# Widening the narrow matmuls of a Fourier, gating and experts kernel to the whole TensorE array

## The chip, the cores and the metric

The kernel runs on one core of a Trainium2 chip. The metric is the device time of one execution in microseconds, from a median over several runs. Engines are named as the profile names them: PE is TensorE's matmul, PEld TensorE's weight load, DVE VectorE, ACT ScalarE, POOL GpSimd and SP SyncE, whose queue issues most of the DMAs.

## The reference, cut to what matters

```python
def reference(x, moe_w1, moe_w2, moe_w3, moe_w_out, moe2_expert_emb, moe2_tau, moe2_w1, moe2_w2):
    X = np.fft.fft(np.fft.fft(x, axis=1), axis=2).real      # x: 8 x 3072 x 256
    t = X.reshape(8 * 3072, 256)
    h = ((t @ moe_w1) * (t @ moe_w2)) @ moe_w3               # 256 -> 1024 -> 1024
    t = h @ moe_w_out                                        # 1024 -> 256
    tn, en = normalised(t), normalised(moe2_expert_emb)
    logits = tn @ en.T / moe2_tau                            # 8 experts
    e = argmax(logits); g = softmax(logits)[e]
    return g * (relu(t @ moe2_w1[e]) @ moe2_w2[e])           # one expert for each token
```

The real part of a 2D transform is symmetric, so half the rows are worked out and the other half follow from sums and differences of the same products.

## The kernel before, in words

Three stages follow one another. Products in float32 are made of three products of split operands: each operand is a high and a low part in the format `fp32r`, and the terms high by high, high by low and low by high are added in PSUM (`three`, `prod`, line 122).

**The transform** (`dft`). For each of 8 batches and 3 parts of the sequence (`KORD`), DVE and POOL fold the rows of `x` to sums and differences, ACT and DVE split them, and PE multiplies them with tables (`accumulate`, tile `acc`). One batch ends with one more term: 2 special rows (`spc`, 2 x 128) times a row of alternating signs (`pm`, 2 x 386). Feature 128, the middle of the spectrum, has no partner and goes the same way for all batches at once (`feature128`): its stationary tiles have 8 columns, one for each batch (`h8`, `l8`, and 2 rows by 8 columns in `x8`). Beside the transform a generator, `side`, prepares the weights; at its end `open_p1` loads the first data of the next stage.

**The middle** (`mid`). 24 chunks of 512 transform columns. A chunk has 8 steps, one for each 128 of the 1024 hidden features (`f`). A step is `stage_b` and `stage_c`. `stage_b` makes four PSUM tiles: `p0`, `q0`, `p1`, `q1`, each of three matmuls of 512 columns. `p1` has a fourth term, a rank-one correction for feature 128: the stationary operand is `wr`, 3 rows by 128 columns of the tile `wrx`, the moving one `ur`, 3 rows by 512 columns. DVE turns the tiles into `ps`, `a`, `b` and `g` (7 instructions a step; for `i` = 1 ACT copies `ps`). `just` splits one block of the chunk before into `jh` (ACT) and `jl` (POOL), and `stage_c` multiplies such a block with `wh` and `wl` (24 matmuls of 264 columns, tile `pc`, one PSUM buffer, which ACT copies to `xs`). Once a chunk, `choose` and `place` work out which expert each token goes to: a chain of some 30 small DVE instructions (`nrm`, `n8q`, `ohot`, `df`, up to `idx`), one ACT instruction (`ex`) and 9 small matmuls; then POOL sends 8 indirect DMAs (`scatter`, `dx`). In the first third, `presplit` also splits the experts' weights (`et`, `eh`, `el`). A small ninth job, `mini`, runs in chunk 0 with 8 matmuls of 3 rows and 8 columns (`umr`).

**The experts** (`experts`): tiles of 256 tokens, each with its expert's weights; nothing of the change lies there.

The order in which instructions stand on each engine is planned ahead of the run by the tile framework, from the order in the text, the tiles' dependences and its own idea of durations; only `experts` has its SyncE order written by hand. So on an engine, work of a later step can stand ahead of an earlier one. Each engine then runs its list in order.

Of the kernel before, what the change touches and what calls it, by code (L numbers as in the profile page):

```python
# [8 lines left out]
F32 = mybir.dt.float32  # L9
F32R = mybir.dt.float32r  # L10
# [8 lines left out]
NB, S, D, F, E = 8, 3072, 256, 1024, 8  # L19
N = NB * S  # L20
H = S // 2
CH = 512
# [37 lines left out]
def fourier_experts(  # L60
# [21 lines left out]
    nc = tc.nc  # L82
# [5 lines left out]
    dspx = tc.dram_tile([NB, 2, 130], F32, name="dspx")  # L88
    du128f = tc.dram_tile([NB, H + 2], F32, name="du128f")
    dwr = tc.dram_tile([3, F], F32, name="dwr")  # L90
# [64 lines left out]
    def load_uv(c, p, raw, pool):  # L155
        b, j = divmod(c, H // CH)
        sl = slice(j * CH, j * CH + CH)
        ru = raw.tile([128, CH], F32, tag="ru", name="ru")
        nc.sync.dma_start(out=ru, in_=du[b, :, sl])
        rv = raw.tile([128, CH], F32, tag="rv", name="rv")  # L160
        nc.sync.dma_start(out=rv, in_=dv[b, :, sl])
        ur = pool.tile([3, CH], F32R, tag=f"ur{p}", name="ur")
        ub = pool.tile([128, CH], F32, tag=f"ub{p}", name="ub")
        nc.sync.dma_start(out=ur[0:1, :].bitcast(F32), in_=du128[b, 0:1, sl])
        nc.sync.dma_start(out=ur[1:3, :].bitcast(F32), in_=du128[b, :, sl])
        nc.sync.dma_start(out=ub, in_=du128f[b:b + 1, sl].to_broadcast([128, CH]))
        return ru, rv, ur, ub
# [3 lines left out]
    def open_p1():  # L171
# [4 lines left out]
        p1["l"] = p1["w"][:, 4 * F:8 * F].rearrange("p (a f) -> p a f", f=F)  # L176
        p1["raw"], p1["uv"] = pool("uvr", left2), pool("uv0", left3)
        ld = load_uv(0, 0, p1["raw"], p1["uv"])
        for q in range(4):
            nc.sync.dma_start(out=p1["h"][:, q, :].bitcast(F32), in_=dwc[0, :, q, :])  # L180
            nc.sync.dma_start(out=p1["l"][:, q, :].bitcast(F32), in_=dwc[1, :, q, :])
        wrx = p1c.tile([128, 4 * XW], F32R, name="wrx")
        p1["wr"] = wrx[0:3, 0:F]
        p1["x"] = wrx.rearrange("p (a c) -> p a c", c=XW)
        nc.scalar.dma_start(out=p1["wr"].bitcast(F32), in_=dwr)
        p1["uh"] = p1c.tile([128, NB], F32R, name="umh")
# [253 lines left out]
def dft(nc, tc, ctx, pz, split, prod, three, x, x128, xsp, tables, p1, du, dv, du128, du128f, dsp, dspx, side):  # L440
# [13 lines left out]
    tl = tb.tile([128, 3, TW], F32R, name="tl")  # L454
    pm = tb.tile([2, 386], F32R, name="pm")

# [31 lines left out]
    load_table(KORD[1], 1)  # L488
    nc.gpsimd.dma_start(out=pm, in_=t_pm)
    ps_ = [wk.tile([128, 4, D + 1], F32, name=f"p{i}_") for i in range(2)]  # L490
# [86 lines left out]
    def fetch_sp(b):  # L577
        if b < NB:
            a = wk2.tile([1, 4, 128], F32, tag="spa", name="spa")
            nc.scalar.dma_start(out=a, in_=dsp[b:b + 1, :, 0:128])  # L580
            c = wk2.tile([2, 128], F32R, tag="spc", name="spc")
            nc.scalar.dma_start(out=c.bitcast(F32), in_=dspx[b, :, 0:128])
            spb[b] = (a, c)
# [7 lines left out]
    def tabs(v, slot, k):  # L591
# [8 lines left out]
        ]  # L600

    def accumulate(ps, rows, v, k, hi, lo, extra, slots=(0, 1, 2, 3)):
        for slot in slots:
            for g, th, tl, w in tabs(v, slot, k):
# [5 lines left out]
                o = ps[g][:rows, 0:w]  # L610
                prod(o, three(hi[:, slot, :], lo[:, slot, :], th, tl), begin, end and extra_ is None)
                if extra_ is not None:
# [11 lines left out]
    def feature128():  # L624
        xm = wk.tile([128, 3, 8, NB], F32, name="xm")
        nc.scalar.dma_start(out=xm, in_=x128)
        x8 = wk.tile([2, NB], F32R, name="x8")
        cm = wk.tile([128, 3, 4, NB], F32, name="cm8")
# [6 lines left out]
        gt(out=um_[:, :, 0, :], in0=dm[:, :, 0, :], in1=dm[:, :, 1, :], op=ALU.add)  # L635
        gt(out=um_[:, :, 1, :], in0=dm[:, :, 0, :], in1=dm[:, :, 1, :], op=ALU.subtract)
        with nc.allow_non_contiguous_dma(reason="a few numbers"):
            nc.sync.dma_start(out=x8.bitcast(F32), in_=dspx[:, :, 128].rearrange("b h -> h b"))
            nc.sync.dma_start(out=um_[0:1, 0, 3, :], in_=dsp[:, 1:2, 128].rearrange("b h -> h b"))
        h8 = wk.tile([128, 3, 4, NB], F32R, name="h8")  # L640
        l8 = wk.tile([128, 3, 4, NB], F32R, name="l8")
        yield
        split(h8, l8, um_, lo_eng=nc.gpsimd)
        yield
        for g, c, w in GROUPS:
            ps = {g: pz.tile([128, 512], F32, tag="z", name="p8")}
            for k in KORD:
                accumulate(ps, NB, 0, k, h8[:, k], l8[:, k], x8)
            n = w + 1 if g == 0 else w
# [21 lines left out]
    for i, (b, k) in enumerate(seq):  # L671
        if k == KORD[0]:
            fetch_sp(b + 1)
            pu = dict(enumerate(banks(4)))
        accumulate(pu, 128, 0, k, *ku.pop(i), spb[b][1])
        if k == KORD[-1]:
# [6 lines left out]
        if k == KORD[0]:  # L683
            pv = dict(enumerate(banks(2)))
        accumulate(pv, 128, 1, k, *kv[i], None, (0, 1))
        if k == KORD[-1]:
# [3 lines left out]
        if k == KORD[-1]:  # L690
            pw = dict(zip((2, 3), banks(2)))
            for q in range(3):
                accumulate(pw, 128, 1, KORD[q], *kv.pop(i - 2 + q), None, (2, 3))
            evacuate(pw, dv, b, GROUPS[2:4])
# [5 lines left out]
def mid(  # L700
# [14 lines left out]

    uvs = [p1["uv"], uv1]
    load_uv = lambda c: p1["load"](c, c % 2, p1["raw"], uvs[c % 2])
    split_uv = lambda c, ld: p1["split"](ld, c % 2, uvs[c % 2])
# [166 lines left out]
    def mini():  # L885
        umr = ro.tile([3, NB], F32R, tag="umr", name="umr")
        umb = ro.tile([128, NB], F32, tag="umb", name="umb")
# [500 lines left out]
```

## Time and profile before

| | |
|---|---|
| median of 3 runs | 2789.34 us (2785.59 to 2789.74) |
| profiled execution, span from first to last instruction | 2776.7 us |
| what lies around the span, median less span | 12.6 us |
| PE busy in the span | 2660.2 us |
| PEld busy in the span | 2411.1 us |
| DVE busy in the span | 1700.2 us |
| rank-one matmuls (3 rows) | 192 |
| special-row matmuls (2 rows) | 8, and 1 in feature 128 |
| matmuls with 8 stationary columns | 54 |

The profile page shows the span, not the whole time of that execution; the 12.6 us is worked out against the median. Busy times of PE are modelled, since matmuls overlap; the distance between the starts of two matmuls says more than their durations. An entry in square brackets in a timeline is the idle time of that engine before the instruction, and who ended it.

### The profile page before, as it was taken

The numbers are of one execution on the slowest core, as the hardware profiler recorded it, in microseconds if no ns is written. First come the engines' busy times: TensorE is split into PE (matmuls) and PEld (weight loads), VectorE is DVE, ScalarE is ACT, GpSimd is POOL, SyncE is SP. The second block draws the span as 40 slices with busy tenths as digits, with TensorE's granted clock in tenths as the row PEclk, the third lists the DMA queues.
The fourth block names the chain that finished last, engine by engine and source line by source line (L and its number), as shares of the span: only waits on it lengthen the run. The fifth ranks groups of instructions, "written<-read, shape, count | busy, mean of one in ns | idle before, by whom it ended". The sixth has DMA issues, their size and how long they took to land. (4 is left out here: it accounts for less than half of the span.)

```text
span 2776.7 us, 48845 instructions
## 1 busy us (share of the span) xinstructions
PE 2660.2 (96%) x18661; PEld 2411.1 (87%) x18661; DVE 1700.2 (61%) x3322; ACT 1054.6 (38%) x2069; POOL 1073.0 (39%) x741
## 2 busy tenths in 40 slices
PE   4998899999999999999999999999999999999998
PEld 3788677777788888878878899999999999999998
DVE  7999399999887887887887762232323222222222
ACT  3554244444434334334333433333333333333332
POOL 5455345565565565565555421111111111111111
PEclk7999799999999999999999999999999999999999
DMA  6766535455111011011010265111111422111110
GB/s 245 245 225 205 186 103 184 153 190 185 58 43 39 28 41 40 28 41 41 28 41 22 99 242 199 47 46 47 47 47 47 164 104 104 47 47 47 47 47 21
DMA packets 114249, 265.07 MB, mean 95 GB/s; under 512 B 16843, under 2 KB 55929, under 8 KB 109148
## 3 DMA queue, kind: packets, MB, share of 16 engines
q1 hardware_dynamic: 84670, 195.58, 21.5%
q0 software_dynamic: 19440, 51.35, 5.2%
q10 hardware_dynamic: 9902, 14.98, 1.5%
q8 instruction: 148, 2.42, 0.4%
q14 instruction: 89, 0.73, 0.1%
HBM read 521.17 MB, written 106.77 MB: 226 GB/s over the span
## 5 line engine op out<-in xcount | busy, mean ns | idle before, releaser
L1071 DVE SCALAR_TENSOR_TENSOR hl<-pd,hh 128x512 fp32r<-128x512 f32 x396 | 273.9, 692 | 779.4 <-ACT hh L1070 779.3
L115 POOL TENSOR_TENSOR jl<-g,jh 128x1024 fp32r<-128x1024 f32 x184 | 441.2, 2399 | 412.9 <-ACT jh L112 334.1
L1086 POOL DMA_INDIRECT out<-o,x x192 | 187.9, 978 | 913.0 <-ACT o L1085 894.4
L122 PE MATMUL pc<-wh,jh 128*128 128x264 f32 x1536 | 441.2, 287 | 15.9 <-ACT xs L799 14.0
L122 PE MATMUL pc<-wh,jl 128*128 128x264 f32 x1536 | 439.2, 286 | 7.4 <-POOL jl L115 7.4
L122 PE MATMUL pc<-wl,jh 128*128 128x264 f32 x1536 | 436.6, 284 | 0.0
L1067 PE MATMUL pd<-xh,wt 128*128 128x256 f32 x2400 | 428.9, 278 | 0.0
L1083 PE MATMUL po<-wt,hh 128*128 128x256 f32 x2400 | 424.1, 280 | 0.0
L112 ACT ACTIVATE jh<-g 128x1024 fp32r<-128x1024 f32 x192 | 203.4, 1059 | 469.9 <-PE pc L122 451.9
L1067 PEld LDWEIGHTS pd<-xh,wt 128*128 128x128 f32 x2400 | 369.2, 188 | 0.0
L1070 ACT ACTIVATE hh<-pd 128x512 fp32r<-128x512 f32 x396 | 237.0, 599 | 336.6 <-PE pd L1067 336.6
L1083 PEld LDWEIGHTS po<-wt,hh 128*128 128x128 f32 x2400 | 364.4, 188 | 0.0
L122 PE MATMUL q<-vh,wc 128*128 128x512 f32 x768 | 326.5, 427 | 13.9 <-ACT a L778 9.5
L1083 PE MATMUL po<-wt,hl 128*128 128x256 f32 x1200 | 334.1, 278 | 0.0
L1067 PE MATMUL pd<-xl,wt 128*128 128x256 f32 x1200 | 333.2, 278 | 0.0
L122 PEld LDWEIGHTS pc<-wh,jh 128*128 128x128 f32 x1536 | 290.4, 189 | 35.3 <-ACT xs L799 26.3
L122 PE MATMUL p<-uh,wc 128*128 128x512 f32 x768 | 307.4, 401 | 3.2 <-DVE ps L765 3.1
L122 PEld LDWEIGHTS pc<-wh,jl 128*128 128x128 f32 x1536 | 289.9, 189 | 12.2 <-POOL jl L115 12.0
L122 PEld LDWEIGHTS pc<-wl,jh 128*128 128x128 f32 x1536 | 290.6, 189 | 6.9
L780 DVE TENSOR_TENSOR b<-ps,q 128x512 f32<-128x512 f32 x384 | 249.0, 688 | 66.0 <-PE q L122 47.6
L783 DVE TENSOR_TENSOR g<-a,b 128x512 f32<-128x512 f32 x384 | 247.4, 679 | 6.3 <-POOL a L780 6.3
L1085 ACT ACTIVATE o<-po,x 128x256 f32<-128x256 f32 x192 | 91.3, 475 | 415.1 <-PE po L1083 415.0
(327 smaller groups left out, 5199.5 us busy)
## 6 DMA issues: line engine op xcount, KB each, us to landing
wt<-dex SPq DMA_DIRECT2D x75, 4096.0 KB
wc<-dex SPq DMA_DIRECT2D x22, 4096.0 KB
x<-dx SPq DMA_DIRECT2D x96, 258.0 KB
xt<-in SPq DMA_DIRECT2D x24, 1028.0 KB
et<-in SPq DMA_DIRECT2D x64, 256.0 KB
dex<-eh SPq DMA_DIRECT2D x64, 256.0 KB
dex<-el SPq DMA_DIRECT2D x64, 256.0 KB
raw<-in SPq DMA_DIRECT2D x28, 512.0 KB
```

What stands on the lines that cost most here:

```text
L112: nc.scalar.activation(out=hi, in_=src, func=AF.Copy)
L115: (lo_eng or nc.vector).tensor_tensor(out=lo, in0=src, in1=hi.bitcast(F32), op=ALU.subtract)
L122: nc.tensor.matmul(ps, lhsT=lh, rhs=rh, start=first and i == 0, stop=last and i == n - 1)
L780: eng.tensor_tensor(out=t, in0=ps, in1=q, op=o)
L783: nc.vector.tensor_tensor(out=gt[sg][:, f, :], in0=ab[0][sg], in1=ab[1][sg], op=ALU.mult)
L1067: nc.tensor.matmul(ps[:, a, :], lhsT=w[:, lh, o:o + 128], rhs=rh[:, k, :], start=i == 0, stop=i == 5)
L1070: nc.scalar.activation(out=hh[:, sl, :], in_=ps, func=AF.Relu)
L1071: nc.vector.scalar_tensor_tensor(out=hl[:, sl, :], in0=ps, scalar=0.0, in1=hh[:, sl, :].bitcast(F32), op0=ALU.max, op1=ALU.subtract)
L1083: nc.tensor.matmul(ps, lhsT=lh[:, f, sl], rhs=w[:, rh, c:c + D], start=i == 0, stop=i == 3 * FT - 1)
L1085: nc.scalar.activation(out=o, in_=ps, func=AF.Copy, scale=x[:, a, D:D + 1].bitcast(F32))
L1086: ins = nc.gpsimd.indirect_dma_start(out=out, out_offset=bass.IndirectOffsetOnAxis(ap=x[:, a, D + 1:D + 2].bitcast(U32), axis=0), in_=o, i ...
```

## The change

The operands of the narrow matmuls become tiles of 128 partitions (or 72 columns) whose rest is zero; the matmuls read them whole. What is computed stays the same.

- `ur`, loaded anew for each chunk, becomes two fixed tiles of 128 x 512 that are set to zero once by POOL; the DMAs write rows 0 to 2 as before. `wrx` is set to zero by POOL before `wr` is loaded into its first three rows, and the matmul reads all 128.
- `pm` and two fixed `spc` tiles of 128 partitions are set to zero by DVE at the start.
- `umr` has 128 partitions and is set to zero by POOL.
- In `feature128` the stationary slices are 72 columns wide: 8 of their own, and 64 that belong to the neighbours or are zero and whose results nobody reads. `x8` is 128 x 72. The tiles `x8`, `h8`, `l8` are set to zero by POOL and reuse other tiles' space.

```diff
@@ load_uv
-        ur = pool.tile([3, CH], F32R, tag=f"ur{p}", name="ur")
+        ur = p1["ur"][p]
@@ open_p1
+        p1["ur"] = [p1["uv"].tile([128, CH], F32R, name="ur0")]
+        nc.gpsimd.memset(p1["ur"][0].bitcast(F32), 0.0)
         ld = load_uv(0, 0, p1["raw"], p1["uv"])
...
         wrx = p1c.tile([128, 4 * XW], F32R, name="wrx")
-        p1["wr"] = wrx[0:3, 0:F]
+        nc.gpsimd.memset(wrx.bitcast(F32), 0.0)
+        p1["wr"] = wrx[:, 0:F]
         p1["x"] = wrx.rearrange("p (a c) -> p a c", c=XW)
-        nc.scalar.dma_start(out=p1["wr"].bitcast(F32), in_=dwr)
+        nc.scalar.dma_start(out=wrx[0:3, 0:F].bitcast(F32), in_=dwr)
@@ dft
-    pm = tb.tile([2, 386], F32R, name="pm")
+    pm = tb.tile([128, 386], F32R, name="pm")
+    nc.vector.memset(pm.bitcast(F32), 0.0)
+    spcs = [tb.tile([128, 128], F32R, name=f"spc{i}") for i in range(2)]
+    for t in spcs:
+        nc.vector.memset(t.bitcast(F32), 0.0)
...
-    nc.gpsimd.dma_start(out=pm, in_=t_pm)
+    nc.gpsimd.dma_start(out=pm[0:2, :], in_=t_pm)
...
-            c = wk2.tile([2, 128], F32R, tag="spc", name="spc")
-            nc.scalar.dma_start(out=c.bitcast(F32), in_=dspx[b, :, 0:128])
+            c = spcs[b % 2]
+            nc.scalar.dma_start(out=c[0:2, :].bitcast(F32), in_=dspx[b, :, 0:128])
@@ accumulate (takes a slice for each slot)
-                prod(o, three(hi[:, slot, :], lo[:, slot, :], th, tl), begin, end and extra_ is None)
+                prod(o, three(hi[slot], lo[slot], th, tl), begin, end and extra_ is None)
@@ feature128
-        x8 = wk.tile([2, NB], F32R, name="x8")
...
+        x8 = wk.tile([128, 72], F32R, tag="cm8", name="x8")
+        nc.gpsimd.memset(x8.bitcast(F32), 0.0)
         with nc.allow_non_contiguous_dma(reason="a few numbers"):
-            nc.sync.dma_start(out=x8.bitcast(F32), in_=dspx[:, :, 128].rearrange("b h -> h b"))
+            nc.sync.dma_start(out=x8[0:2, 0:NB].bitcast(F32), in_=dspx[:, :, 128].rearrange("b h -> h b"))
...
-        h8 = wk.tile([128, 3, 4, NB], F32R, name="h8")
-        l8 = wk.tile([128, 3, 4, NB], F32R, name="l8")
+        wide = [wk.tile([128, 11 * NB + 72], F32R, tag=t, name=f"{n}8") for n, t in (("h", "xm"), ("l", "l8"))]
+        for t in wide:
+            nc.gpsimd.memset(t.bitcast(F32), 0.0)
+        h8, l8 = (t[:, 0:12 * NB].rearrange("p (k s b) -> p k s b", k=3, s=4) for t in wide)
...
+        cols = lambda t, k: {s: t[:, (4 * k + s) * NB:(4 * k + s) * NB + 72] for s in range(4)}
...
-                accumulate(ps, NB, 0, k, h8[:, k], l8[:, k], x8)
+                accumulate(ps, 72, 0, k, cols(wide[0], k), cols(wide[1], k), x8)
@@ mid
+    p1["ur"].append(uv1.tile([128, CH], F32R, name="ur1"))
+    nc.gpsimd.memset(p1["ur"][1].bitcast(F32), 0.0)
@@ mini
-        umr = ro.tile([3, NB], F32R, tag="umr", name="umr")
+        umr = ro.tile([128, NB], F32R, tag="umr", name="umr")
+        nc.gpsimd.memset(umr.bitcast(F32), 0.0)
```

## Rows read from the trace of the kernel before

**Rows 1.** Page, part 1: busy us (share of the span) and instructions of each engine.

```profile
PE 2660.2 (96%) x18661; PEld 2411.1 (87%) x18661; DVE 1700.2 (61%) x3322; ACT 1054.6 (38%) x2069; POOL 1073.0 (39%) x741
```

**Rows 2.** Windows: us, busy PE, PEld, DVE, ACT, POOL (x instructions), clock, DMA share, GB/s.

```profile
0.00:303.30 303.30, 241.11 (x1257) 219.19 (x1258) 256.94 (x481) 134.50 (x259) 158.98 (x95) 0.89 0.69 231
303.30:357.70 54.40, 45.01 (x165) 32.42 (x163) 28.07 (x63) 14.53 (x27) 23.76 (x22) 0.78 0.39 132
357.70:743.80 386.10, 368.89 (x2135) 300.65 (x2134) 358.98 (x674) 175.16 (x362) 208.94 (x124) 0.99 0.48 155
743.80:1527.20 783.40, 772.29 (x4576) 636.44 (x4575) 641.52 (x1296) 312.02 (x643) 441.37 (x269) 1.00 0.11 35
...
1576.00:2776.70 1200.70, 1184.91 (x10248) 1182.79 (x10247) 372.93 (x715) 400.56 (x742) 213.72 (x218) 1.00 0.24 82
```

**Rows 3.** PE timeline: first rank-one matmuls of chunks 8 and 23 (start, us).

```profile
743.82 0.50 PE L122 MATMUL p<-ur,wrx 3*128 3x512 f32 x1
...
1527.21 0.50 PE L122 MATMUL p<-ur,wrx 3*128 3x512 f32 x1
```

**Rows 4.** Waits of DVE in chunks 8 to 22 (us in total, times, longest).

```profile
DVE ps L765 <- PE p L122: 88.0, 75, 1.7
```

**Rows 5.** Waits of PE in the same chunks 8 to 22.

```profile
PE pc L122 <- ACT xs L799: 6.7, 15, 0.5
PE pc L122 <- POOL jl L115: 4.4, 15, 0.3
```

**Rows 6.** PE timeline around one rank-one matmul of chunk 9 (start, us).

```profile
801.82 0.39 PE L122 MATMUL p<-ul,wc 128*128 128x512 f32 x1
802.05 0.40 PE L122 MATMUL p<-uh,wc 128*128 128x512 f32 x1
802.38 0.50 PE L122 MATMUL p<-ur,wrx 3*128 3x512 f32 x1
802.80 0.50 PE L122 MATMUL q<-vh,wc 128*128 128x512 f32 x1
803.14 0.39 PE L122 MATMUL q<-vl,wc 128*128 128x512 f32 x1
```

**Rows 7.** Groups by form, PEld: busy, mean ns, idle before and what ended it.

```profile
L122 PEld LDWEIGHTS p<-ur,wrx 3*128 3x128 f32 x192 | 34.9, 182 | 69.9 <-issue 67.4 <-DMA rv<-dv 2.5
```

**Rows 8.** Groups by form, PE: the rank-one, special-row and feature 128 matmuls.

```profile
L122 PE MATMUL p<-ur,wrx 3*128 3x512 f32 x192 | 96.0, 500 | 0.0
...
L122 PE MATMUL acc<-pm,spc 2*128 2x386 f32 x8 | 4.0, 500 | 0.0
...
L122 PE MATMUL p<-th,h 128*8 128x384 f32 x15 | 5.0, 336 | 2.0 <-DVE wcl L115 1.7 <-ACT r L652 0.3
```

**Rows 9.** DVE timeline of chunk 13: three instructions of choose and place.

```profile
1017.18 1.90 DVE L138 SCALAR_TENSOR_TENSOR n8q<-n8q,ss 128x8 f32<-128x8 f32 x1
...
1023.22 2.23 DVE L834 TENSOR_TENSOR df<-df,inv 128x64 f32<-128x64 f32 x1
...
1027.91 0.16 DVE L860 CAST idx<-sl 128x8 uint32<-128x8 f32 x1
```

**Rows 10.** POOL timeline of chunk 13: three subtractions and the first scatter.

```profile
1016.68 2.39 POOL L115 TENSOR_TENSOR jl<-g,jh 128x1024 fp32r<-128x1024 f32 x1 [3.91 <-ACT jh L112]
1022.99 2.38 POOL L115 TENSOR_TENSOR jl<-g,jh 128x1024 fp32r<-128x1024 f32 x1 [3.93 <-PE p L122]
1028.35 1.00 POOL L864 DMA_INDIRECT dx<-xs,idx  x1 [2.98 <-DVE idx L860]
...
1037.09 2.40 POOL L115 TENSOR_TENSOR jl<-g,jh 128x1024 fp32r<-128x1024 f32 x1
```

**Rows 11.** Waits of DVE in chunks 1 to 7.

```profile
DVE ps L765 <- PE p L122: 4.8, 4, 2.0
...
DVE b L780 <- PE q L122: 2.3, 4, 0.6
```

**Rows 12.** POOL timeline at the start of the middle: the kernel's own memset.

```profile
303.82 0.96 POOL L895 MEMSET hm<- 128x1024 f32 x1
```

More of the change, by code (lines that the diff above doesn't have):

```diff
@@ L600, in tabs, with by_slot @@
         ]
+    def by_slot(hl):
+        return [{s: t[:, s, :] for s in range(4)} for t in hl]
     def accumulate(ps, rows, v, k, hi, lo, extra, slots=(0, 1, 2, 3)):
@@ L674, in dft @@
             pu = dict(enumerate(banks(4)))
-        accumulate(pu, 128, 0, k, *ku.pop(i), spb[b][1])
+        accumulate(pu, 128, 0, k, *by_slot(ku.pop(i)), spb[b][1])
         if k == KORD[-1]:
@@ L684, in dft @@
             pv = dict(enumerate(banks(2)))
-        accumulate(pv, 128, 1, k, *kv[i], None, (0, 1))
+        accumulate(pv, 128, 1, k, *by_slot(kv[i]), None, (0, 1))
         if k == KORD[-1]:
@@ L692, in dft @@
             for q in range(3):
-                accumulate(pw, 128, 1, KORD[q], *kv.pop(i - 2 + q), None, (2, 3))
+                accumulate(pw, 128, 1, KORD[q], *by_slot(kv.pop(i - 2 + q)), None, (2, 3))
             evacuate(pw, dv, b, GROUPS[2:4])
```

## The prediction

> **What bounds the kernel now.** I read the page first: PE is busy 96% of the span, DVE 61% [rows 1]. An average over three stages proves little, so the second view is the table of windows [rows 2]. The experts (1576 on) are PE alone, 1185 of 1201 us, and nothing of the change lies there. The transform (0 to 303) has DVE busier than PE, 257 against 241 us. The middle falls into three parts. Chunk 0 (303 to 358) leaves PE 9 of 54 us idle. Chunks 1 to 7 have DVE busy 359 of 386 us, 93%, because the experts' weights are split there too. Chunks 8 to 22 have PE busy 772 of 783 us and DVE 642, 82%. The 192 rank-one matmuls are spread evenly over the middle, 8 a chunk, and 128 of them lie in chunks 8 to 23, where PE looks like the limit.
>
> How much of PE there is a limit? The starts of the first rank-one matmul of chunks 8 and 23 [rows 3] give (1527.21 - 743.82) / 15 = 52.23 us a chunk. In those 15 chunks DVE waits 75 times for `p` [rows 4], 5 of 8 steps: there PE sets the pace and DVE follows. In the other three steps DVE carries `choose` and `place` as well and does not wait. PE itself waits twice a chunk [rows 5]: once for ACT to empty `pc` (6.7 us over 15, 0.45 each) and once for POOL's `jl` (4.4 us, 0.29 each). Those two waits are small now, and they are what a faster PE runs into.
>
> **What one narrow matmul costs.** The timeline around one of them [rows 6] has matmuls of 512 columns start 0.23 us apart (801.82 to 802.05). With the narrow one between, the starts are 0.33, 0.42 and 0.34 apart: from 802.05 to 803.14 it is 1.09 us for three steps that would take 3 x 0.23 = 0.69. So it costs 0.40 us over an ordinary matmul of the same length, before it, in it and after it. The load of its weights tells where: 182 ns long, but in total 69.9 us of idle stand before the 192 loads, 0.36 us each, 67.4 of them ended by "issue", that is, by nothing the profile shows [rows 7]. Between ordinary matmuls 0.23 us apart there is no room for such a wait, so their loads run under the matmul before; this one does not start until that matmul is well through, and the next full one waits again.
>
> [...]
>
> After the change I price a rank-one matmul at 0.23 us, the ordinary step; from below, a gain cannot exceed 0.40 + 0.23 (the matmul gone), and from above, the price stays 0.63 if the cause is another. I take 0.23, since the widened instruction has exactly the form of its neighbours in [rows 6].
>
> **Chunks 8 to 23.** 8 x 0.40 = 3.2 us of PE time a chunk go away, but not all of it can be kept. In chunk 13, the DVE chain of `choose` runs without a gap from step 1 to step 3. Two of its small instructions are long: `n8q`, 128 x 8, takes 1.90 us and ends at 1019.08; `df` takes 2.23 and ends at 1025.45 [rows 9]. POOL's subtractions `jl` end at 1019.07 and 1025.37 [rows 10]. So these DVE instructions are held until POOL's subtraction is over. Each `jl` follows `jh`, which follows PE's `stage_c` of that step: it moves with PE. Hence the chain shortens with PE in part: `n8q` ends one saving (0.40) earlier by step 1, `df` two savings earlier by step 2, and after `df` nothing on the way to `idx` depends on PE. From `idx` at 1027.91 POOL sends seven scatters and only then does the `jl` of 1037.09, which ends at 1039.49 [rows 10] and which PE awaits in step 5.
>
> So between step 1 and step 5 PE saves 5 x 0.40 = 2.0, but what it waits for comes 2 x 0.40 = 0.8 earlier; the other 1.2 us turns into wait: `jl` grows from 0.29 to about 1.1, `xs` from 0.45 to about 0.85 on the way (the latter is contained in the former's sum). Steps 6, 7 and 0 are PE's own: 3 x 0.40 = 1.2. Together 0.8 + 1.2 = 2.0 us a chunk, 16 x 2.0 = 32 us. Bounds: 16 x 1.2 = 19 if the chain does not shorten at all, 16 x 3.2 = 51 if neither wait grows.
>
> **Chunks 1 to 7.** Full saving would be 7 x 3.2 = 22 us, but DVE has only 27 us of idle in 386 [rows 2], most of it behind ACT's split of the experts' weights. What DVE waits for PE is 4.8 + 2.3 = 7.1 us [rows 11]; a faster PE can take no more than about that. I take 4, bounds 0 and 7.1.
>
> **Chunk 0 and the mini job.** 8 rank-one matmuls and 8 of 3 x 8: 16 x 0.40 = 6.4 at most (an estimate by the price of the 512-column one), in a stretch where PE idles. I take 1, bounds 0 and 4.
>
> **The transform.** The 8 special-row matmuls last 500 ns, as the rank-one ones do [rows 8]; 8 x 0.40 = 3.2 us of PE, in a stretch where DVE has more to do. The 54 matmuls with 8 columns last 336 ns for 384 columns [rows 8] and follow each other, so only the ends of their four groups could cost: 8 changes of form at no more than 0.20, 1.6 us. I take 1 for both, bounds 0 and 4.8.
>
> **What is added.** POOL's memset of 128 x 1024 takes 0.96 us [rows 12]. By that `ur` is 0.5 twice, `wrx` 1.0, the others under 0.2 each (estimates by columns). The zeros for `ur` and `wrx` stand at the end of the preparation, where the tile's space comes free; the loads that now wait for them (SP: `ur`, behind it `ub` and the 8 loads of `wc`; ACT: `wr`) are used first in chunk 0. POOL has 144 us without work in the transform [rows 2]. If the memset stood in POOL's list ahead of a fold and waited there for its space, `vl` and PE behind it would lose that wait, an estimate of up to 2 us. DVE's three memsets at the start lie before the first data. I count nothing, with a loss of 2 in the bounds. No DMA is added; POOL's `pm` load now follows a DVE memset and is needed only at the end of the first batch.
>
> **The sum.** 32 + 4 + 1 + 1 = 38 us. The profile's span of 2776.7 becomes 2738.7; with the 12.6 that the median lies above the span, 2789.3 becomes 2751. By the bounds: 19 - 2 = 17 less gives 2772; 51 + 7.1 + 4 + 4.8 = 67 less gives 2722.
>
> **Rivals.**
> First, PE keeps all of it in chunks 8 to 23: 51 + 7 + 2 + 2 = 62, **2727**. For it: both waits of PE are now under half a microsecond [rows 5], and DVE is at 82%. Against: seven scatters and a subtraction stand between `idx` and PE, and no PE time is in them. Chance 0.16.
>
> Second, the widening does nothing: the gap is tied to the fourth term itself (its tile, its place), not to its rows; **2789**. For it: "issue" names no cause [rows 7], and the narrow operands lie in tiles that no other matmul reads. Against: the special rows, with other tiles, show the same 500 ns. Chance 0.03. [...]
>
> Third, the chain does not shorten: `n8q` and `df` fall ahead of the subtraction or wait as long as now. 19 + 4 + 1 + 1 = 25, **2764**. Chance 0.13.
>
> Fourth, slower: with PE 0.4 us a step ahead, POOL's subtractions fall on other instructions of `choose`. One more hold of a whole subtraction, 2.4 us a chunk, eats the 2.0 (16 x 0.4 = 6 us lost, 6 gained elsewhere: no change, chance 0.03). Two more holds give 16 x (4.8 - 2.0) = 45 lost less 6, **2828**. It decides from 2.4 us of further hold a chunk on. For it: two holds of 1.9 and 2.2 us stand there now by mere timing [rows 9]. Against: the holds in the way move with PE, and the chain has but two or three subtractions beside it. Chance 0.07.
>
> **How the numbers follow.** Forecast 0.58 at 2751, own range 2740 to 2760. First rival 0.16 and third 0.13 make 0.87 faster. No change (within 0.2%, about what a measurement of this kernel can tell) 0.03 + 0.03 = 0.06; slower 0.07. The range 2722 to 2772 holds the forecast and both faster rivals and is the bounds' own.
>
> **What would show it.** Right: the load of `ur` without idle before it, starts 0.23 apart through it; steps 0.4 us shorter where DVE waits for PE; a chunk of about 50.2 us; PE's waits for `jl` grown to some 1.1 us a chunk; chunks 1 to 7 shorter by well under 1 us each. Wrong: idle still before that load; or another order of instructions on DVE or POOL, planned anew because of the memsets and fixed tiles, which moves the holds and the scatters; or a new wait of POOL near 270 us.

## The result, and the profile after

The changed kernel takes 2762.53 us (median of 4 runs, 2756.8 to 2768.9) against 2789.54 for the kernel before (4 runs, 2785.59 to 2798.07): a ratio of 0.9902, with a 95% interval of 0.9879 to 0.9926. So 27.0 us are gone (20.6 to 33.8 by the interval), where 38 were forecast.

The two profiles stand closer together than the medians. That of the changed kernel is of an execution of 2768.9 us, 6.4 above its median, with a span of 2767.2; in its runs the span lies 1.7 to 1.8 us below the time. The span of 2776.7 of before then belongs to an execution of about 2778.5 us (an estimate by the same 1.8), 11.0 below its median. The spans are only 2776.7 - 2767.2 = 9.5 us apart, the medians 27.0. Stages are read from the profiles, the effect from the medians.

First the page of the changed kernel, part 1: busy time of each engine, its share, instructions.

```profile
PE 2602.1 (94%) x18661; PEld 2441.5 (88%) x18661; DVE 1690.8 (61%) x3325; ACT 1049.5 (38%) x2069; POOL 1078.0 (39%) x748
```

PE works 58 us less than in [rows 1], and the span is only 9.5 us shorter. PE has become idle. The windows of the changed kernel say where (columns as in [rows 2]: transform, chunk 0, chunks 1 to 7, chunks 8 to 22, experts).

```profile
0.00:304.00 304.00, 234.71 (x1256) 217.55 (x1257) 255.29 (x484) 134.88 (x259) 162.06 (x100) 0.91 0.69 231
304.00:355.90 51.90, 41.62 (x165) 32.43 (x165) 26.97 (x63) 14.85 (x27) 24.27 (x24) 0.80 0.44 138
355.90:744.00 388.10, 355.34 (x2135) 308.28 (x2134) 355.28 (x674) 173.42 (x362) 209.69 (x124) 0.97 0.47 154
744.00:1512.30 768.30, 735.21 (x4576) 654.98 (x4575) 635.04 (x1296) 308.79 (x643) 441.84 (x269) 0.99 0.11 36
1559.00:2767.20 1208.20, 1191.27 (x10265) 1188.98 (x10263) 374.96 (x719) 400.40 (x743) 215.19 (x219) 1.00 0.24 82
```

Chunks 8 to 22 went from 783.4 to 768.3 us, 15.1 less, 51.2 a chunk. Chunks 1 to 7 became 2.0 longer, and what follows chunk 22 5.4 (1254.9 against 1249.5), though of the change only chunk 23 lies there. PE's idle time in chunks 8 to 22 rose from 783.4 - 772.3 = 11.1 to 768.3 - 735.2 = 33.1 us.

Next the price of one rank-one matmul. The load of its weights, and the three widened kinds of matmul, in the groups by form of the changed kernel, answer to [rows 7, 8].

```profile
L122 PEld LDWEIGHTS p<-ur,wrx 128*128 128x128 f32 x192 | 36.5, 190 | 8.0
...
L122 PE MATMUL p<-ur,wrx 128*128 128x512 f32 x192 | 76.7, 399 | 0.0
...
L122 PE MATMUL p<-th,h 128*72 128x384 f32 x15 | 5.9, 392 | 2.7 <-DVE wcl L115 1.7 <-ACT r L666 1.0
...
L122 PE MATMUL acc<-pm,spc 128*128 128x386 f32 x8 | 2.9, 364 | 0.0
```

The idle time ahead of the load fell from 69.9 to 8.0 us. The PE timeline around one of them, in chunk 13 of the changed kernel (start, us), shows starts 0.23 us apart all the way through, where [rows 6] had 0.33, 0.42 and 0.34.

```profile
1026.77 0.39 PE L122 MATMUL p<-ul,wc 128*128 128x512 f32 x1
1027.00 0.39 PE L122 MATMUL p<-uh,wc 128*128 128x512 f32 x1
1027.23 0.39 PE L122 MATMUL p<-ur,wrx 128*128 128x512 f32 x1
1027.46 0.39 PE L122 MATMUL q<-vh,wc 128*128 128x512 f32 x1
1027.68 0.39 PE L122 MATMUL q<-vl,wc 128*128 128x512 f32 x1
```

Then PE's waits in chunks 8 to 22 of the changed kernel (us in total, times, longest), beside [rows 5].

```profile
PE pc L122 <- ACT xs L815: 32.4, 26, 2.5
PE pc L122 <- POOL jl L115: 0.2, 1, 0.2
```

They rose from 11.1 to 32.6 us. Both the name and the length matter: not `jl` but ACT's copy `xs`, and up to 2.5 us at a time. Four chunks of the 15 look as forecast, one of them chunk 13. In it, the held instructions of DVE and the subtractions of POOL are these (timelines of the changed kernel, DVE, then POOL):

```profile
1014.06 1.53 DVE L138 SCALAR_TENSOR_TENSOR n8q<-n8q,ss 128x8 f32<-128x8 f32 x1
...
1019.71 1.81 DVE L850 TENSOR_TENSOR df<-df,inv 128x64 f32<-128x64 f32 x1
1023.98 0.16 DVE L876 CAST idx<-sl 128x8 uint32<-128x8 f32 x1
```

```profile
1013.12 2.43 POOL L115 TENSOR_TENSOR jl<-g,jh 128x1024 fp32r<-128x1024 f32 x1 [3.49 <-ACT jh L112]
1019.03 2.40 POOL L115 TENSOR_TENSOR jl<-g,jh 128x1024 fp32r<-128x1024 f32 x1 [3.48 <-PE p L122]
1024.42 0.98 POOL L880 DMA_INDIRECT dx<-xs,idx  x1 [2.98 <-DVE idx L876]
...
1033.11 2.40 POOL L115 TENSOR_TENSOR jl<-g,jh 128x1024 fp32r<-128x1024 f32 x1
```

`n8q` ends at 1015.59 and `df` at 1021.52, with the subtractions (1015.55 and 1021.43), as in [rows 9, 10]. The chunk's first rank-one matmul starts at 1002.11, so `jl` ends 33.40 us into the chunk; before, the same interval was 1039.49 - 1004.95 = 34.54. PE waits 0.89 and 1.00 us in this chunk (both times for `xs`, where the forecast had `jl` the second time), and it lasts 50.14 us; 9, 19 and 21 last 50.14 to 50.17. That is the forecast 50.2.

Other chunks last up to 52.7. Every third chunk (8, 11, 14, 17, 20), `choose` deals with the first chunk of a batch and has one instruction more: the one-hot is multiplied by `val`, which is 0 for padding. These are the masked chunks. Chunk 14 of the changed kernel, DVE's timeline:

```profile
1063.41 2.41 DVE L846 TENSOR_TENSOR ohot<-ohot,val 128x64 bf16<-128x64 bf16 x1
...
1069.97 1.77 DVE L831 TENSOR_SCALAR nrm<-nrm 128x8 f32<-128x8 f32 x1
...
1072.48 0.23 DVE L850 TENSOR_TENSOR df<-df,inv 128x64 f32<-128x64 f32 x1
```

And POOL, ACT and PE in the same chunk:

```profile
1063.35 2.40 POOL L115 TENSOR_TENSOR jl<-g,jh 128x1024 fp32r<-128x1024 f32 x1 [3.54 <-ACT jh L112]
1069.30 2.41 POOL L115 TENSOR_TENSOR jl<-g,jh 128x1024 fp32r<-128x1024 f32 x1 [3.56 <-PE p L122]
...
1072.74 0.26 ACT L851 ACTIVATE ex<-df 128x64 f32<-128x64 f32 x1 [3.51 <-DVE df L850]
...
1073.33 0.46 PE L122 MATMUL pc<-wh,jh 128*128 128x264 f32 x1 [1.76 <-ACT xs L815]
```

The multiplication starts 0.06 us after the subtraction and is held to its end. In the kernel before, the same two instructions of the same chunk stand the other way round (DVE, then POOL):

```profile
1068.58 0.23 DVE L830 TENSOR_TENSOR ohot<-ohot,val 128x64 bf16<-128x64 bf16 x1
```

```profile
1068.91 2.39 POOL L115 TENSOR_TENSOR jl<-g,jh 128x1024 fp32r<-128x1024 f32 x1 [3.94 <-ACT jh L112]
```

There it was done 0.1 us before the subtraction began. Now the long instructions in this chunk are 2.41 + 1.77 us, in place of 1.53 + 1.81 in the unmasked chunk 13; `df` comes later, `ex` with it, and on ACT the copy of `pc` stands behind `ex`: ACT is idle for 3.51 us until `df`, `ex` starts at 1072.74 and the copy at 1072.90. PE waits 1.76 us for that copy, and 2.46 in chunks 11 and 17.

In chunks 13 and 14 all four long instructions end within 0.1 us of a subtraction of POOL (`ohot` at 1065.82 beside 1065.75, `nrm` at 1071.74 beside 1071.71). `ohot`, `n8q` and `df` have two tensor inputs and lasted up to 2.41 us; `nrm`, which lasted 1.77 us, has one. What ties the two engines is not shown beyond these times.

After this wait PE also runs slower. Windows of the changed kernel from before the wait of chunk 14 to after it (clock is the third column from the right):

```profile
1066.00:1069.00 3.00, 3.00 (x31) 2.86 (x30) 2.97 (x9) 0.83 (x1) 0.00 (x0) 1.00 0.00 0
...
1072.00:1075.00 3.00, 1.68 (x8) 1.68 (x9) 3.00 (x14) 1.53 (x5) 0.00 (x0) 0.75 0.00 0
1075.00:1079.00 4.00, 4.00 (x23) 3.81 (x23) 2.96 (x8) 0.99 (x2) 2.79 (x3) 0.76 0.19 66
1079.00:1082.00 3.00, 3.00 (x18) 2.60 (x17) 2.62 (x5) 1.46 (x5) 2.10 (x3) 1.00 0.25 88
```

Between 1073.3 and 1076.9 the matmuls of 264 columns start 0.22 apart, later 0.12: the granted clock is 0.53 there, and 1.00 from 1077 to 1079. So step 3 of this chunk lasts 9.5 us, against 7.05 in an unmasked one. Over the 3.5 us from just after the wait the clock is 0.51 here, and 0.53 to 0.67 behind the longest waits of chunks 8, 11, 12, 17 and 20 (1.76 to 2.46 us); behind those in step 5 of chunks 10, 15, 16, 18 and 22 (1.56 to 1.71 us) it is 1.00.

### The profile page after: what moved, and what is told of

Its sections match the earlier page's. It is cut to its first block, busy times and chain, and to the rows that moved or that the text cites. A ratio compares the mean times of both kernels' runs of the same rounds, so it can differ in the third digit from the quotient of the medians.

```text
span 2767.2 us, 48866 instructions
## 1 busy us (share of the span) xinstructions
PE 2602.1 (94%) x18661; PEld 2441.5 (88%) x18661; DVE 1690.8 (61%) x3325; ACT 1049.5 (38%) x2069; POOL 1078.0 (39%) x748
## 4 chain that ended last, share of the span: by engine, by line
issue 39%; PE 27%; DVE 17%; POOL 11%; DMA 3%; ACT 2%; POOLq 0%; SPq 0%; DVEq 0%; ACTq 0%
PE pc L122 14%; POOL out L1103 7%; PE p L122 6%; PE q L122 5%; DVE b L796 2%; DVE g L799 2%; POOL vl L115 2%; DMA et<-in 2%; DVE a L796 2%; PE acc L122 1%; DVE ps L781 1%; DVE el L115 1%; ACT jh L112 1%; DVE nrm L139 1%; POOL z L504 1%
## 5 line engine op out<-in xcount | busy, mean ns | idle before, releaser
L122 PE MATMUL pc<-wh,jh 128*128 128x264 f32 x1536 | 449.9, 293 | 53.1 <-ACT xs L815 50.4
L122 PE MATMUL pc<-wl,jh 128*128 128x264 f32 x1536 | 442.7, 288 | 0.0
L122 PEld LDWEIGHTS pc<-wh,jh 128*128 128x128 f32 x1536 | 296.4, 193 | 82.4 <-ACT xs L815 73.3
L122 PE MATMUL q<-vh,wc 128*128 128x512 f32 x768 | 308.0, 403 | 17.2 <-ACT a L794 10.6
L122 PEld LDWEIGHTS pc<-wl,jh 128*128 128x128 f32 x1536 | 296.9, 193 | 5.8
L122 PEld LDWEIGHTS pc<-wh,jl 128*128 128x128 f32 x1536 | 295.9, 193 | 5.6 <-POOL jl L115 5.4
L880 POOL DMA_INDIRECT dx<-xs,idx x192 | 192.5, 1003 | 154.3 <-DVE idx L876 82.0
```

Source lines behind the costliest of these rows:

```text
L122: nc.tensor.matmul(ps, lhsT=lh, rhs=rh, start=first and i == 0, stop=last and i == n - 1)
L880: i = nc.gpsimd.indirect_dma_start(out=dx, out_offset=bass.IndirectOffsetOnAxis(ap=idx[:, j if k is None else k:][:, 0:1], axis=0), in_=xs ...
```

## The experiments

Each run stands beside runs of the kernel before that were made with it: 2789.89 us (13 runs) for the first four, 2780.18 (10 runs) for the next four, 2781.88 (7 runs) for the last four.

**1. Only the rank-one rows.** The kernel before, with `ur`, `wrx` and `umr` widened and nothing else.

```diff
+        p1["ur"] = [p1["uv"].tile([128, CH], F32R, name="ur0")]
+        nc.gpsimd.memset(p1["ur"][0].bitcast(F32), 0.0)
...
-        p1["wr"] = wrx[0:3, 0:F]
+        nc.gpsimd.memset(wrx.bitcast(F32), 0.0)
+        p1["wr"] = wrx[:, 0:F]
...
```

> Only the rank-one rows of the middle and of its mini job are widened; the transform keeps its narrow matmuls. My theory: 192 drains of 0.40 us are nearly the whole effect, so the time is that of the full change, 2760 to 2768 us, ratio to before about 0.990, and the load of ur has no idle before it. Rival: the special rows and feature 128 carry a good part (they lie in a stretch where PE is idle part of the time, but each miss may cost a clock drop); then 5 us or more of the gain is missing, 2770 or above.

Measured: 2759.43 us (2758.14 to 2766.31, 4 runs), ratio 0.9902, interval 0.9885 to 0.9918. That is the ratio of the whole change. The drains of this expectation, and of that of run 8, are the 0.40 us of [rows 6]; that anything is drained in them is shown by no run. In this run too the masked chunks 11 and 17 have a step 3 of 10.1 and 10.2 us.

**2. Only the transform.** The opposite half: special rows and feature 128 widened, the rank-one matmul reads 3 rows as before.

```diff
-        ur = p1["ur"][p]
+        ur = pool.tile([3, CH], F32R, tag=f"ur{p}", name="ur")
...
-        p1["wr"] = wrx[:, 0:F]
+        p1["wr"] = wrx[0:3, 0:F]
...
```

> Only the special rows and feature 128 are widened; the middle keeps its 3-row matmuls. My theory: within 0.2% of before, at most 3 us gained, since DVE is busier than PE in that stretch. Rival: 5 us or more gained, 2784 or below.

Measured: 2785.25 us (2781.48 to 2791.91, 10 runs), ratio 0.9982, interval 0.9972 to 0.9991: 4.6 us less, between 2.5 and 7.8 by the interval; that is more than my 3 and less than the rival's 5, and decides between neither. It does not add to the first run visibly, and in the profile of the whole change the transform is no shorter (first rank-one matmul at 306.28, before 305.54). Where these few us lie was not located.

**3 and 4. How many rows make a matmul narrow?** The changed kernel, whose rank-one matmul reads 64 or 72 rows of the same zeroed tiles. Everything else, memsets and fixed tiles too, is the same in both.

```diff
-        p1["wr"] = wrx[:, 0:F]
+        p1["wr"] = wrx[0:64, 0:F]
...
-                terms.append((wr[:, fs], ur))
+                terms.append((wr[:, fs], ur[0:64, :]))
...
```

> The full change, but the rank-one matmuls read 64 rows in place of 128 (zeros beyond 3 as before). If the cost belongs to a change of the array's form between 64 and 128 rows, the load of ur again stands behind 0.36 us of idle and its matmul's neighbours start 0.33, 0.42 and 0.34 us apart, and the time is that of the kernel before. Rival: only very few rows are slow, and 64 rows run as 128 do: starts 0.23 apart.

> The full change, but the rank-one matmuls read 72 rows. If the form is chosen by rows and 72 rounds up to the whole array, the load runs under the matmul before it (idle near 0) and starts are 0.23 us apart, as with 128 rows, time near 2763. Rival: every row count other than that of the neighbours costs the 0.40, and the time is that of the kernel before.

Measured, one run each: 2788.57 us with 64 rows, 2753.57 with 72. The groups by form of the weight loads, of the run with 64 rows and of the one with 72:

```profile
L122 PEld LDWEIGHTS p<-ur,wrx 64*128 64x128 f32 x192 | 35.2, 183 | 69.9 <-issue 68.1 <-DMA rv<-dv 1.8
```

```profile
L122 PEld LDWEIGHTS p<-ur,wrx 72*128 72x128 f32 x192 | 36.4, 189 | 7.9
```

With 64 rows the idle time ahead of the load is the 69.9 us of [rows 7] to the tenth; with 72 rows it is gone. The starts around the matmul are 0.33, 0.43 and 0.34 us apart with 64 rows, 0.23 with 72. Neither the zeros nor the tiles are the cause, then, but the number of rows that the instruction names, with the border between 64 and 72.

So 64 rows cost what 3 rows do, and 72 cost nothing; no count between them was run. What happens in the 0.40 us is not shown: three distances are longer, ahead of the matmul, at it and behind it, and no run changes the neighbours.

**5. Spread the scatters.** The changed kernel, with each scatter queued on POOL behind the subtraction of its own step, so that the `jl` which PE awaits in step 5 no longer stands behind seven scatters.

```diff
...
-                            scatter(pend[0], idx, j)
+                            with tc.issue_after(jl[0]):
+                                scatter(pend[0], idx, j)
```

> The full change, and each scatter queued on POOL behind the subtraction jl of its own step, so that no jl stands behind seven scatters. My theory: PE's wait in step 5 of each chunk (1.0 to 1.8 us) goes, worth about 1.3 us in each of 16 chunks and some clock drops: 2735 to 2750 us. Rival: that wait comes from something else (ACT's order, DVE), and another wait takes its place: within 5 us of the full change.

Measured: 2750.54 us (2748.23 to 2753.8, 4 runs), ratio 0.9892, interval 0.9868 to 0.9916. The wait in step 5 is gone: one wait a chunk stays, by the chain of waits of chunks 8 to 22 in this run.

```profile
PE pc L122 <- ACT xs L817: 18.8, 15, 2.5
```

Step 5 lasts 5.9 us, unmasked chunks 48.8 to 49.1, chunks 8 to 22 together 1493.32 - 747.05 = 746.3. Four of the five masked chunks keep a step 3 of 9.5 to 10.2; in chunk 14 it lasts 8.0, with the granted clock at 1.00 behind the same wait of 1.76 us. The total is just above the 2735 to 2750 us expected, and the kernel before that was run beside it takes 9.4 us less as well (2780.18 against 2789.54): by the ratios, the gain over the changed kernel (0.9902) can't be told from none.

**6. The gate later.** The changed kernel, with `ex` and the gate's sum queued on ACT behind the copy `xs` of the step, instead of ahead of it.

```diff
...
+                        with tc.issue_after(out_c[0]):
+                            gate()
                         idx = place(*sel)
```

> The full change, and ex, the exponential of choose, queued on ACT behind the copy xs of that step, so that xs no longer waits for DVE's chain. My theory: PE's wait for xs in step 3 (0.8 to 2.5 us) goes, and with it the drop of the clock behind it in one chunk of three; but step 5 waits for POOL as long as before, and POOL's scatters follow DVE's chain, so most comes back there: 2745 to 2760 us. Rival: all of it comes back in step 5, within 3 us of the full change.

Measured: 2764.98 us (2763.0 to 2770.75, 5 runs), ratio 0.9948, interval 0.9928 to 0.9967. PE's longest wait in chunks 8 to 22 of this run has changed its name:

```profile
PE pc L122 <- POOL jl L115: 35.0, 15, 2.7
```

Step 3 falls to 5.9 in unmasked chunks (7.1 at most in masked ones), and step 5 rises to 8.3 to 10.4. All that step 3 gives comes back in step 5, because the seven scatters and the `jl` behind them keep their time. The rival was right, and in total the run is if anything worse than the changed kernel: 0.9948 against 0.9902, with intervals that just fail to meet (0.9928 and 0.9926).

**7 and 8. Both reorderings, wide and narrow.** Runs 5 and 6 together, on the changed kernel and on the kernel before.

> The full change with both reorderings. My theory: nothing in chunks 8 to 23 is left for PE to wait on, and a chunk takes 8 steps of 5.9 us and some 0.5 us for place, about 48.5 us in place of 51.2: 2715 to 2735 us, and the clock stays up. Rival: DVE, now at 88 to 90% there, becomes the limit, and a chunk stays at 50 us or more: 2745 or above.

> Both reorderings in the kernel before, with its narrow matmuls. My theory: PE waited only 0.74 us a chunk there, so at most 16 x 0.74 = 12 us and some of the waits of chunks 1 to 7 are to be had: 2770 to 2785 us, and the distance to the same reorderings with the wide matmuls is some 50 us, the 3.2 us a chunk of the drains. Rival: the reorderings are worth the same with narrow and with wide matmuls, and the distance stays at 27 us.

Measured: wide 2724.68 us (2720.95 to 2727.32, 4 runs), ratio 0.9797, interval 0.9773 to 0.9821; narrow 2770.31 (2767.61 to 2774.6, 6 runs), ratio 0.9962, interval 0.9948 to 0.9977. The windows of chunks 8 to 22, of the wide run and then of the narrow one:

```profile
745.60:1466.40 720.80, 719.08 (x4577) 647.99 (x4576) 633.11 (x1296) 308.46 (x643) 443.29 (x269) 1.00 0.12 38
```

```profile
752.70:1516.80 764.10, 764.10 (x4577) 636.55 (x4576) 640.31 (x1296) 310.18 (x643) 442.37 (x269) 1.00 0.11 36
```

PE is busy nearly all the time in both, and the two differ by 43.3 us in 15 chunks, 2.9 a chunk of the 3.2 that the price gives. Both times came as expected (their distance was put at some 50 us). Without the two waits the widening is worth 2770.31 - 2724.68 = 45.6 us; with them, by the medians of the result, 27.0.

**9. The mask by a memset.** The changed kernel, in which the padding's entry of the one-hot is set to zero by a memset of 1 x 4 words instead of the multiplication of the whole one-hot.

```diff
-        if masked:
+        if masked and nt < 8:
             nc.vector.tensor_tensor(
                 out=oh[:, :nt], in0=oh[:, :nt], in1=val[:, t0:t0 + nt].unsqueeze(2).to_broadcast(sh), op=ALU.mult
             )
+        elif masked:
+            nc.vector.memset(oh[0:1, 4:5, :], 0.0)
```

> The full change, but in every third chunk the multiplication of ohot with a mask (128 x 64, two SBUF operands, 2.41 us there) is replaced by zeroing the one row of the one token that it masks, which reads nothing. My theory: such a multiplication is held by POOL's subtraction, and it is what makes chunks 8, 11, 14, 17, 20 and 23 late: their step 3 falls from 8.0 to 10.2 us to about 7.1, as in the chunks without mask, some 10 us in all. Rival: what the multiplication does not wait for, the next instruction of the chain does, and step 3 stays at 8 us or more in at least half of these chunks.

Measured: 2753.13 us, one run. All chunks from 8 to 22 last 50.12 to 50.38 us, the masked ones too, with a step 3 of 7.04 to 7.08. The DVE timeline of chunk 14 of this run, then the windows and PE's waits of chunks 8 to 22:

```profile
1059.71 0.06 DVE L850 MEMSET ohot<- 1x4 uint32 x1
...
1060.50 1.59 DVE L138 SCALAR_TENSOR_TENSOR n8q<-n8q,ss 128x8 f32<-128x8 f32 x1
...
1066.22 1.87 DVE L852 TENSOR_TENSOR df<-df,inv 128x64 f32<-128x64 f32 x1
```

```profile
747.10:1500.90 753.80, 725.25 (x4577) 647.69 (x4576) 628.43 (x1296) 310.31 (x643) 441.60 (x269) 1.00 0.11 36
```

```profile
PE pc L122 <- POOL jl L115: 15.7, 15, 1.1
PE pc L122 <- ACT xs L815: 12.8, 15, 0.9
```

This is the forecast chunk, row by row: 753.8 / 15 = 50.25 us, `jl` 1.05 and `xs` 0.85 a chunk. With the multiplication gone, so is the extra hold, and the clock is 1.00 throughout. The 10 us expected are not shown in the total: one run at 2753.13 is 0.9897 of its kernel before, and the changed kernel has 0.9902.

**10. Work instead of a wait.** The changed kernel, where PE in step 3 of a masked chunk repeats three matmuls of `q` twice more, 6 x 0.23 = 1.4 us of work that overwrites the same result, in the place of idle time. It asks what makes step 3 long there, the wait itself or the lower clock behind it.

```diff
             prod(pq, features(i, 1, f, (vh, vl), "v"))
+            if i == 1 and f == 3 and c >= 2 and (c - 2) % (H // CH) == 0:
+                for _ in range(2):
+                    prod(pq, features(i, 1, f, (vh, vl), "v"))
```

> The full change with work added: in step 3 of every third chunk (those with mask) the three matmuls of q1 are done three times over, 6 matmuls of 0.23 us or 1.4 us more, just ahead of where PE waits for xs. [...]

Measured: 2765.82 us, one run. Step 3 of the masked chunks lasts 8.0 (8, 14, 20) or 8.6 (11, 17) in place of 9.5 or 10.0 to 10.2, although it holds 1.4 us more work, and the granted clock stays at 1.00 there, where the changed kernel has 0.51 to 0.67 behind its wait. In chunk 14 it falls in step 5 instead, by the windows of this run:

```profile
1072.00:1075.00 3.00, 3.00 (x15) 2.41 (x14) 2.90 (x6) 2.44 (x5) 2.09 (x4) 1.00 0.27 94
...
1083.00:1087.00 4.00, 3.47 (x16) 3.47 (x17) 0.61 (x2) 0.00 (x0) 2.78 (x2) 0.57 0.00 0
```

Step 5 of these chunks grew to 8.5 to 9.9: POOL issues eight scatters ahead of the `jl` in them, where the changed kernel has seven, 1.3 us more, and PE waits 2.2 to 2.4 us there. So with that wait filled (0.35 us of it is left in chunk 14) the clock did not fall in step 3. But a wait did not always bring a fall: of the five in step 5, only that of chunk 14 did. Nor was time won: steps 3 and 5 together last 16.4 to 17.9 us, against 15.8 to 16.5 in the changed kernel. A faster step 3 of a masked chunk runs into the scatters, as in run 6.

**11 and 12. The best version.** Both reorderings, with the scatters spread from chunk 8 on only (chunks 1 to 7 had lost by it: 745.62 - 353.25 = 392.4 us in run 7, against 388.1), and then with the mask by a memset as well.

```diff
...
+                            with tc.issue_after(jl[0]) if c >= 8 else ExitStack():
...
```

> Both reorderings, but the scatters are spread only from chunk 8 on; in chunks 2 to 6, where DVE is the limit, spreading had lengthened step 4 (from 5.9 to 7.5 or 8.1 us). My theory: those chunks return to 53 to 55.5 us each and the time falls by 5 to 10 us, to 2714 to 2720 (from 2724.7). Rival: what step 4 gains comes back in step 5, which waits for the scatters as before: within 3 us of 2724.7.

> Both reorderings from chunk 8 on, and the mask by a memset. My theory: chunks 11, 17 and 23 lose the 1.1 us that their step 3 still has over the others, the other masked ones 0.4 us: 3 to 5 us less than the reorderings alone, 2711 to 2716. Rival: no difference beyond 2 us, since the hold passes to the next instruction.

Measured: 2719.46 us (2709.99 to 2720.08, 4 runs), ratio 0.9767, interval 0.9746 to 0.9787; with the memset 2711.51 (2709.87 to 2716.32, 4 runs), ratio 0.9747, interval 0.9731 to 0.9764. Chunks 1 to 7 take 387.5 us in the first. In the second, PE has no wait in chunks 8 to 22, whose window is

```profile
741.60:1459.10 717.50, 717.50 (x4577) 648.26 (x4576) 627.53 (x1296) 308.61 (x643) 443.00 (x269) 1.00 0.12 38
```

47.8 us a chunk, all of it PE; in the run without the memset these 15 chunks take 720.7 us. That is the 3 us expected of it; the intervals of the two totals overlap. This version is 2.5% faster than the kernel before, and faster than the changed one.

## Why the prediction was right, and where it was too large

The forecast was 2751 and the range 2722 to 2772; the median is 2762.5. The mechanism was right; two terms were mis-sized, what is kept in chunks 8 to 23 and what is kept in chunks 1 to 7. The median lies outside the narrower range of 2740 to 2760 that I gave the forecast.

**The price, 0.40 us.** Right: starts 0.23 us apart through the widened matmul, and PE's work in chunks 8 to 22 without any fall of the clock (run 9) is 772.3 - 725.25 = 47.0 us less, 3.1 a chunk against 3.2 forecast. Runs 3 and 4 show what it hangs on, the number of rows. The second rival (the widening does nothing) is out.

**What is kept, 2.0 us a chunk.** This is the larger mis-sized term. Its working holds for the chunks that it was worked out on: in run 9, 47.0 us of work are saved, waits grow from 11.1 to 28.5, and 15 chunks are 783.4 - 753.8 = 29.6 us shorter, 1.97 each. But I took one chunk, 13, for all, and every third is masked. In the profiled run 15.1 us were saved, 1.0 a chunk. The difference from run 9, 14.5 us, is 735.2 - 725.25 = 10.0 us of PE work at a lower clock and 33.1 - 28.5 = 4.6 of further waiting. It lies mostly in the masked chunks: 8, 11, 14, 17 and 20 are together 9.1 us over 50.25 each, chunk 12 (a wait of 1.84 us in step 5, then a granted clock of 0.66 over 3.5 us) 2.5, and 10, 15, 16, 18 and 22 some 3.3. In those last ones PE waits for `xs` in step 5, 1.6 to 1.7 us.

That wait in step 5 does not come from the change. In ACT's list `jh` stands ahead of `xs`. ACT's timeline in chunk 10, of the changed kernel and then of run 9:

```profile
878.62 1.06 ACT L112 ACTIVATE jh<-g 128x1024 fp32r<-128x1024 f32 x1 [6.25 <-PE q L122]
```

```profile
876.87 1.06 ACT L112 ACTIVATE jh<-g 128x1024 fp32r<-128x1024 f32 x1 [2.97 <-PE pc L122]
```

In run 9 `jh` starts as the last matmul of step 4's `pc` ends (it starts at 876.61); in the changed kernel that matmul starts at 875.08 and `jh` follows 3.3 us after its end. Such a late start, by 1.3 to 3.5 us, stands in all of chunks 8 to 22 of the changed kernel and of runs 1 to 4, narrow or wide; in the profile of before and in runs 5 to 12 it is never above 0.3. Its cause is open. So the two main profiles differ in something that is not the change, and 1.0 a chunk is too low. Two pairs are alike in it: the kernel before and run 9 give 1.97 a chunk, without the mask's hold; runs 3 and 4, 790.9 and 764.6 us for the 15 chunks, give 1.75 with it, 2.2 in unmasked chunks and 0.9 in masked ones. The second is what the term measures: 28 us in 16 chunks in place of 32, and what is missing is lost in the masked chunks.

**The fourth rival** (the subtractions fall on other instructions of `choose`, 2.4 us a time) was priced for every chunk and given 0.03 with one hold more and 0.07 with two. It happened in part: one hold more in one chunk of three, on an instruction that had escaped by 0.1 us. It is not a separate case beside the forecast but a share of it.

**The chain behind `df`.** Right. `jl` of step 5 ends 33.40 us into chunk 13 instead of 34.54: 1.14 earlier, close to the 3 x 0.40 of steps 0 to 2 (the forecast's 0.8, and the 0.40 of step 0, since the chunk is counted from its first rank-one matmul). That the seven scatters are the rest of it is shown by runs 5 to 8: only without both waits does the widening bring 2.9 us a chunk. The first rival (all is kept, 2727) needs both reorderings.

**The third rival** (the chain does not shorten, 2764) has the number nearest to the median, by chance: the chain did shorten, and 1.75 a chunk are kept, not its 1.2.

**Chunks 1 to 7, 4 us.** Wrong, nothing was kept: 2.0 us longer in the profile, and 385.5 with 72 rows (run 4) against 383.3 with 64 (run 3). In the profile chunk 1 alone lost 3.2 (63.0 against 59.9), again by a hold: by DVE's and PE's timelines of chunk 1 of the changed kernel,

```profile
382.50 2.30 DVE L139 SCALAR_TENSOR_TENSOR nrm<-nrm,n1q 128x1 f32<-128x1 f32 x1
384.73 0.15 DVE L846 TENSOR_TENSOR ohot<-ohot,val 128x8 bf16<-128x8 bf16 x1
```

```profile
384.93 0.17 PE L863 MATMUL pr<-ohot,tri 128*128 128x16 bf16 x1 [2.90 <-DVE ohot L846]
```

a `nrm` of one column starts 0.06 us after a subtraction of POOL (382.44) and is held with it (they end at 384.80 and 384.78; this `nrm` otherwise takes 0.15 us); `ohot` and PE's `pr` wait behind. Before, that wait of PE was 0.38 us. The hold alone undoes what the chunk gains elsewhere: in runs 1 and 4 the same wait of 2.9 leaves the granted clock at 1.00, and the chunk lasts 60.1. In the changed kernel's profile the clock is 0.81 over steps 2 and 3, which is the rest. Chunks 2 to 7 gained 1.1. One reading behind this term was wrong too: of the 27 us in which DVE is idle there, 9.2 are behind ACT's split of the experts' weights, not most.

**Transform 1, chunk 0 1, memsets 0.** Chunk 0 became 2.6 us shorter in the profile and 3.1 between runs 3 and 4 (52.4 and 49.3), so about 3, within my bound of 4. The transform became 0.7 longer in the profile, while run 2 puts its part at 2.5 to 7.8 us; with wide special rows the first rank-one matmul starts anywhere from 298.5 to 307.5 us in these traces, so this term stays unjudged. The 0.20 us for each change of form in it, half of the 0.40, was the author's estimate and is shown by no run: in the trace of before, the starts into, through and out of a group of 8 columns are 0.17 to 0.18 us apart (121.71 to 125.20), as those of the full matmuls beside it are. PE's wait for `vl` at the end of the transform is 0.6 us as before (0.7), and POOL's memset of `ur` waits 16.6 where another memset waited 16.4: nothing came with the memsets. Without the transform the terms now add up to 28 + 3 + 0 = 31 us, within the 20.6 to 33.8 of the result; the forecast's 38 is not.

**The 12.6 us "around the span".** Wrong as a reading, though it did not change the sum: 1.8 us lie around the span, and the rest is that the profiled execution differs from those of the median. In runs 2 and 3, narrow too, a chunk lasts 52.7 us, not 52.23, and step 5 7.3, not 6.9: they have the late `jh`. That fits the medians of the kernel before, 2789.9 us beside runs 1 to 4 and 2780 to 2782 beside runs 5 to 12; but there is no trace of the kernel before itself with a late `jh`, so this is argued and not shown.

## What to carry to other kernels

The lone matmul over 3 rows between full ones cost 0.40 us more than an ordinary step of 0.23; the idle time ahead of its weight load, ended by "issue", told so (69.9 us before 192 loads), and rows of zeros took it away (8.0 us). When an engine that sets the pace becomes faster, list the short instructions of VectorE that stand beside a long one of GpSimd, with the time between their starts: where it is a tenth of a microsecond, a hold of the whole long instruction may move to a worse place (`ohot` in chunk 14: done 0.1 us ahead of the subtraction before, held for 2.41 us after), and it must be looked up in every kind of iteration, not in one. Of two waits in one chain, the first can give its gain back in the second (run 6); both together were worth most (run 7). And before two profiles are compared, look for a wait that differs between them and that the change does not touch.

## What the runs showed of the hardware that was not expected

- The border between 64 and 72 rows: 69.9 us of idle time ahead of 192 weight loads at 64 rows, as with 3, and 7.9 at 72.
- A VectorE operation with a single tensor input (`nrm`, 128 x 8, usually 0.16 us) was held for 1.77 us, to the end of a GpSimd subtraction (1071.74 beside 1071.71 in chunk 14).
- The granted clock after a wait of PE: 0.75 after the 1.76 us of chunk 14 and 0.57 after the 2.26 us of step 5 in run 10, but 1.00 after 1.76 us in chunk 8 of run 1 and after 2.2 to 2.4 us in four chunks of run 10. In run 9, with no wait over 1.1 us, it is 1.00 in all of chunks 8 to 22. What tells the waits apart was not settled. In the changed kernel's profile the falls cost about 10 us of PE time in 15 chunks.
- ACT's `jh`, which in nine of the profiled kernels starts within 0.3 us of the end of the PE product ahead of it, starts 1.3 to 3.5 us after it in all of chunks 8 to 22 of the other five (the changed kernel and runs 1 to 4), with 3, 64, 72 and 128 rows alike. Its cause is open.
